# A spatial product in 2 x 3 by 3 x 3 blocks by 15 products instead of 2 x 2 by 7, with its sums of blocks of v accumulated in DRAM

## The chip, the core and the metric

The kernel runs on one core of a Trainium2 chip. The metric is the device time of one launch in microseconds (us), as the median of several runs. The profile is of one execution, and its times count from that execution's first instruction.

## The reference

There are three stages, of which the last holds the change. The first is the real part of a two-dimensional Fourier transform of `x` (4 batches, 3072 positions, 256 features). The second is a feed-forward layer with 2048 hidden features. The third is a gated layer in which positions are mixed:

```python
h = np.maximum(x @ w_in, 0.0)
u, v = (h[..., : d_ff // 2], h[..., d_ff // 2 :])          # 512 columns each
mu = np.mean(v, axis=-1, keepdims=True)
var = np.mean((v - mu) ** 2, axis=-1, keepdims=True)
v_n = (v - mu) / np.sqrt(var + 1e-06)
v_s = np.einsum('ts,bsd->btd', w_spatial, v_n) + b_spatial[None, :, None]
gated = u * v_s
return (gated @ w_out).astype(np.float32)
```

`w_spatial` is 3072 x 3072 and `v_n` is 3072 x 512 per batch. This "spatial product" is the largest piece of work of the kernel.

## The kernel before

**Three matmuls for one.** TensorE multiplies float32 operands that are split in two parts, `hi` (12 significant bits) and `lo` (the rest). `matmul3` (L160) issues three matmuls, hi by hi, hi by lo and lo by hi (L162 to L164). ScalarE makes `hi` by a copy (L829) and VectorE makes `lo` by a subtraction (L835).

**Fourier and feed-forward stages.** After the Fourier transform (L166 to L395) the loop at L721 walks over 16 blocks of 768 positions (4 batches of 4 blocks) in 8 steps each. Beside the matmuls of a block, the pieces of the block before are run: a `v_piece` (L631) makes 128 rows of v_n, a `u_piece` (L680) makes u, and both go to DRAM. A block has six v pieces, run one per step in the first six steps. For a v piece ScalarE applies the rectifier and sums the row (L658), GpSimd takes the mean (L660), ScalarE sums the squared deviations (L665), six small GpSimd instructions make 1/sqrt(var) (L666 to L671), and VectorE normalizes in place (`norm`, L674). The normalized tile is stored a step later by `run_norms` (L708): one DMA of 256 KB, issued by ScalarE (L710). Within `run_norms` the stores of the step before stand ahead of the new norms. For the last block the mean and the variance come from VectorE (L654, L655); its pieces are run by `finish` (L766) after the loop, among the first operands of the spatial product. Four buffers hold the v tiles.

**The spatial product.** Two batches make a pair. The product of a pair is cut into 2 x 2 blocks and done by seven products of sums of blocks (`PRODUCTS`, L38). Each product is made of units (L786): one unit is two blocks of 128 rows of s, one chunk `c` of 512 columns of t and all four blocks `j` of 128 features, 24 matmuls of 128x512. There are 2 pairs x 7 products x 3 chunks x 6 steps `p` = 252 units. Each unit needs its operand w, and each head `(product, p)` needs an operand v that all its chunks use.

An operand is made in steps that are written into the units ahead of its use: `load` (L807, SyncE, 512 KB per term into one of 7 `raw` buffers), `add` (L820, VectorE, one instruction per further term), `high` (ScalarE) and `low` (VectorE). For w they stand three, two, two and one units ahead (`operands`, L931). All engines work their queues in order, and SyncE goes on to the next load as soon as a `raw` buffer is free.

After the last step of a chunk, `collect` (L867) adds or subtracts its four accumulators (`sacc`) into the sums that the product belongs to, one VectorE instruction per accumulator and sum. Complete sums are multiplied by u (`gate_high`), split, and multiplied by w_out (`project`, L894) one block of 128 features at a time, in two PSUM banks of their own.

Of the kernel before, what the change touches and what calls it, by code (L numbers as in the profile page):

```python
# [13 lines left out]
ALU = mybir.AluOpType  # L14
# [23 lines left out]
PRODUCTS = [  # L38
# [7 lines left out]
]  # L46

# [29 lines left out]
def tables():  # L77
    """Twiddles of the folded transforms, by the shapes alone."""
# [31 lines left out]
def fourier_ffn_gated_kernel(ctx: ExitStack, tc: tile.TileContext, t, out: bass.AP):  # L110
# [7 lines left out]
    v_d = [[dram.tile([P, 6, HV], F32, name=f"v{b}{c}") for c in range(4)] for b in range(B)]  # L118
# [41 lines left out]
    def matmul3(acc, w, x, start, stop):  # L160
        """acc += w.T @ x from the split operands w = (hi, lo), x = (hi, lo)."""
        nc.tensor.matmul(acc, lhsT=w[0], rhs=x[0], start=start, stop=False)  # L162
        nc.tensor.matmul(acc, lhsT=w[0], rhs=x[1], start=False, stop=False)  # L163
        nc.tensor.matmul(acc, lhsT=w[1], rhs=x[0], start=False, stop=stop)  # L164

# [1 line left out]
    with ExitStack() as ph:  # L167
        pool = lambda n, **k: ph.enter_context(tc.tile_pool(name=n, reuse_waits="tile", **k))  # noqa: E731
# [48 lines left out]
        def rows384(b):  # L217
            """ce, so, co and se of row 384, in that order."""
# [29 lines left out]
        def row0(b):  # L248
            """Row 384 takes the rows that a sine of zero leaves free."""
# [5 lines left out]
        def lhs(b, sl):  # L255
            """The operands of the products along the sequence."""
# [374 lines left out]
    def v_piece(i, k):  # L631
# [461 lines left out]
```

## Time and profile before

| | |
|---|---|
| time of three runs | 2812.86, 2813.70 and 2813.86 us, median 2813.7 |
| span of the profiled execution, first to last instruction | 2809.1 us |
| what the median of the runs has beyond that span | 4.6 us |
| busy: PE, VectorE, ScalarE, GpSimd | 97%, 73%, 46%, 16% of the span |
| DMA: moved, mean rate | 438.91 MB, 156 GB/s |

The profile gives the profiled execution's span; its own time on the device's clock stands nowhere beside it, so the sum below is made against the span, and the 4.6 us around it are taken as unchanged. Busy shares are means over stages that differ much: the Fourier stage fills the first 200 us or so, the feed-forward stage goes to about 1276 us, and the spatial product from 1295 us to the end. GpSimd is busy in the first two stages alone.

### The profile page before, as it was taken

Reading aid. Unit: us, or ns where it says so; the run is one execution under the profiler, and the core shown is the slowest. Engines: PE = TensorE matmul, PEld = TensorE weight load, DVE = VectorE, ACT = ScalarE, POOL = GpSimd, SP = SyncE. Lnnn points to the kernel's source line nnn. Section 1 sums busy time; section 2 is a strip of 40 time slices with the busy share of each in tenths; the row PEclk is TensorE's granted clock in tenths of the full one; section 3 lists DMA queues with packets and bytes.
Section 4 is the critical chain, followed back from the end, with each engine's and each line's share of the span. In section 5 each row is a group of like instructions: output and inputs, shape, how many; then the busy total and the mean of one; then the engine's idle time right before and its main releaser. Section 6 shows DMA issues by size and latency. Waiting matters only on the chain.

```text
span 2809.1 us, 34578 instructions
## 1 busy us (share of the span) xinstructions
PE 2728.8 (97%) x13142; PEld 2410.1 (86%) x13142; DVE 2052.4 (73%) x2509; ACT 1301.6 (46%) x1652; POOL 453.8 (16%) x791
## 2 busy tenths in 40 slices
PE   5867999999999999999999999999999999999999
PEld 5757999999999999998888888888888888888887
DVE  8878888888888888886677665577645777646764
ACT  3455777777777777774323222233222232223332
POOL 5367222232222222222000000000000000000000
PEclk8979999999999999999999999999999999999999
DMA  5521111111111111117577775577746777736773
GB/s 226 174 80 42 54 58 54 57 54 60 57 58 54 57 58 54 49 64 273 171 254 247 262 257 173 188 241 265 257 165 195 242 262 261 245 131 230 249 255 118
DMA packets 158744, 438.91 MB, mean 156 GB/s; under 512 B 17753, under 2 KB 50538, under 8 KB 156914
## 3 DMA queue, kind: packets, MB, share of 16 engines
q1 hardware_dynamic: 122440, 380.04, 39.9%
q10 hardware_dynamic: 36138, 56.68, 5.5%
q8 instruction: 102, 1.67, 0.2%
q14 instruction: 64, 0.52, 0.1%
HBM read 367.41 MB, written 69.25 MB: 155 GB/s over the span
## 4 chain that ended last, share of the span: by engine, by line
PE 91%; DVE 4%; POOL 2%; DMA 1%; ACT 1%; issue 1%; ACTq 0%; SPq 0%; POOLq 0%; DVEq 0%
PE sacc L164 16%; PE sacc L163 16%; PE sacc L162 16%; PE acc L163 6%; PE acc L164 6%; PE acc L162 6%; PE po L163 3%; PE po L164 3%; PE po L162 3%; PE pu L162 2%; PE pu L164 1%; PE pu L163 1%; PE pv L164 1%; PE pe L163 1%; PE pe L164 1%; PE pe L162 1%
## 5 line engine op out<-in xcount | busy, mean ns | idle before, releaser
L164 PE MATMUL sacc<-whi,vlo 128*128 128x512 f32 x2016 | 786.9, 390 | 0.0
L162 PE MATMUL sacc<-whi,vhi 128*128 128x512 f32 x2016 | 784.9, 389 | 1.1 <-ACT uu L695 1.1
L163 PE MATMUL sacc<-wlo,vhi 128*128 128x512 f32 x2016 | 785.9, 390 | 0.0
L835 DVE TENSOR_TENSOR wlo<-raw,whi 128x1024 fp32r<-128x1024 f32 x252 | 308.6, 1224 | 489.0 <-PE sacc L163 321.1
L829 ACT CAST whi<-raw 128x1024 fp32r<-128x1024 f32 x252 | 265.1, 1052 | 586.9 <-DVE raw L823 440.2
L162 PEld LDWEIGHTS sacc<-whi,vhi 128*128 128x128 f32 x2016 | 378.5, 188 | 82.0 <-ACT uu L695 1.5
L163 PEld LDWEIGHTS sacc<-wlo,vhi 128*128 128x128 f32 x2016 | 378.3, 188 | 80.8
L164 PEld LDWEIGHTS sacc<-whi,vlo 128*128 128x128 f32 x2016 | 378.3, 188 | 79.3
L163 PE MATMUL acc<-glo,wo1h 128*128 128x384 f32 (+1 forms) x1024 | 350.4, 342 | 20.7 <-POOL glo L588 14.7
L162 PE MATMUL acc<-ghi,wo1h 128*128 128x384 f32 (+1 forms) x1024 | 348.5, 340 | 0.0
L164 PE MATMUL acc<-ghi,wo1l 128*128 128x384 f32 (+1 forms) x1024 | 348.4, 340 | 0.0
L588 DVE TENSOR_TENSOR glo<-h,ghi 128x1536 fp32r<-128x1536 f32 (+3 forms) x128 | 218.8, 1710 | 135.7 <-ACT ghi L581 135.7
L823 DVE TENSOR_TENSOR raw<-raw 128x1024 f32<-128x1024 f32 x240 | 288.3, 1218 | 0.0
L886 ACT CAST gh<-sum 128x512 fp32r<-128x512 f32 (+1 forms) x97 | 59.9, 618 | 380.0 <-DVE sum L884 380.0
L574 DVE SCALAR_TENSOR_TENSOR h<-e,h 128x1536 f32<-128x1536 f32 (+1 forms) x128 | 231.9, 1811 | 0.0
L563 ACT ACTIVATE e<-h 128x1536 f32<-128x1536 f32 (+1 forms) x128 | 190.0, 1485 | 87.7 <-DVE h L555 82.1
L163 PEld LDWEIGHTS acc<-glo,wo1h 128*128 128x128 f32 x1024 | 195.0, 190 | 25.5 <-POOL glo L588 17.1
L581 ACT CAST ghi<-h 128x1536 fp32r<-128x1536 f32 (+1 forms) x128 | 187.7, 1466 | 20.0 <-DVE h L574 20.0
L164 PEld LDWEIGHTS acc<-ghi,wo1l 128*128 128x128 f32 x1024 | 195.2, 191 | 0.0
L162 PEld LDWEIGHTS acc<-ghi,wo1h 128*128 128x128 f32 x1024 | 194.6, 190 | 0.1
L568 ACT ACTIVATE e<-e 128x1536 f32<-128x1536 f32 (+1 forms) x128 | 190.2, 1486 | 0.0
L554 DVE TENSOR_TENSOR h<-q,po 128x384 f32<-128x384 f32 (+1 forms) x256 | 142.1, 555 | 36.2 <-POOL glo L588 8.3
(196 smaller groups left out, 4141.7 us busy)
## 6 DMA issues: line engine op xcount, KB each, us to landing
raw<-in_wT SPq DMA_DIRECT2D x432, 512.0 KB, 4.6
raw<-v SPq DMA_DIRECT2D x144, 512.0 KB, 4.7
u<-uu ACTq DMA_DIRECT2D x128, 192.0 KB, 1.9
v<-v ACTq DMA_DIRECT2D x96, 256.0 KB, 2.9
u<-u SPq DMA_DIRECT2D x16, 1024.0 KB
q<-in_xq SPq DMA_DIRECT2D x12, 1032.0 KB
out<-sum SPq DMA_DIRECT2D x48, 256.0 KB, 2.1
u<-u SPq DMA_DIRECT2D x16, 512.0 KB, 4.4
```

The source lines that it names most:

```text
L162: nc.tensor.matmul(acc, lhsT=w[0], rhs=x[0], start=start, stop=False)
L163: nc.tensor.matmul(acc, lhsT=w[0], rhs=x[1], start=False, stop=False)
L164: nc.tensor.matmul(acc, lhsT=w[1], rhs=x[0], start=False, stop=stop)
L554: v.tensor_tensor(h[:, z, :n], q[:, :n], po[:, :n], op=ALU.add)
L563: nc.scalar.activation(e[:, :, :w], st[s]["h"][:, :, :w], AF.Relu, scale=-1.0)
L568: nc.scalar.activation(e[:, :, :w], e[:, :, :w], AF.Exp, scale=-1.0)
L574: nc.vector.scalar_tensor_tensor(out=h[:, :, :w], in0=e[:, :, :w], scalar=-1.0, in1=h[:, :, :w], op0=ALU.add, op1=ALU.max)
L581: nc.scalar.copy(st[s]["hi"][:, :, :w], st[s]["h"][:, :, :w])
L588: eng.tensor_tensor(st[s]["lo"][:, z, :w], st[s]["h"][:, z, :w], st[s]["hi"][:, z, :w].bitcast(F32), op=ALU.subtract)
L823: nc.vector.tensor_tensor(x, x, y, op=ALU.add if sg > 0 else ALU.subtract)
L829: nc.scalar.copy(hi, x)
L835: nc.vector.tensor_tensor(lo, x, hi.bitcast(F32), op=ALU.subtract)
```

## The change

The spatial product of a pair (2 batches by 3072 s by 3072 t) is cut into thirds of s and of t, not halves, and done by 15 products where 18 would be the plain number. A product now has 2 chunks of 512 columns and 4 steps, so a pair has 120 units, and both pairs 240.

- The table names for each product: a first and a second set of v blocks (blocks 0 to 2 are the thirds of the first batch, 3 to 5 of the second), the signed blocks of w, the sums that read the accumulator, and whether it continues on the accumulators that the product before left in PSUM ("running sums"). The products have 1, 3, 1, 2, 3, 1, 3, 1, 2, 3, 1, 3, 1, 2 and 2 terms of w.
- `V_SETS` are the 14 sets of v blocks that occur. Their sums are no longer made from loaded blocks: every normalized v tile is stored into each set that its block belongs to, five of them. The first block of a set is stored by SyncE, the others by GpSimd with an accumulating DMA. Of 480 stores of 256 KB, 224 are plain and 256 accumulate. Blocks 0 to 5 have 0, 3, 2, 3, 3 and 5 accumulating stores per tile.
- An operand v is then one load (two in the 14th product).
- The eight PSUM banks are the accumulators of the two chunks. `project` takes two banks of the chunk that is not being worked on, does all four blocks of features at once, and is put only where those banks hold no running sum (`idle`).
- There are 8 `raw` buffers in place of 7, loads stand one unit earlier (`LEAD`), the v operands have 5 buffers of each part and not 8, 11 buffers hold sums and u, and u is loaded by GpSimd. The bias is loaded in 24 pieces of 256 KB.

```diff
-VB = 8
+VB = 5
+KP = NT // 6
+MC = NCH // 3
...
 PRODUCTS = [
-    ([(1, 1, 0), (1, 1, 1)], [(1, 0, 0)], [(1, 1, 0), (-1, 1, 1)]),
...
+    ((1, 2, 4, 5), (), [(1, 1, 0)], [(1, 0, 0)], False),
+    ((1,), (), [(1, 1, 1), (-1, 0, 1), (-1, 1, 0)], [(1, 0, 1)], True),
+    ((4, 5), (), [(1, 2, 1)], [(1, 1, 1)], False),
+    ((2, 4, 5), (), [(1, 1, 0), (-1, 2, 1)], [(-1, 0, 1)], True),
+    ((2,), (), [(1, 0, 0), (1, 2, 1), (-1, 2, 0)], [(-1, 0, 0), (1, 1, 0)], True),
...
 ]
+NR = len(PRODUCTS)
+V_SETS = sorted({x for q in PRODUCTS for x in q[:2] if x})
...
         def norm():
             nc.vector.tensor_scalar(v, v, mean, y, op0=ALU.subtract, op1=ALU.mult)
-            stores.append((v_d[b][c][:, k], v))
+            third, at = divmod(6 * c + k, 2 * KP)
+            e = 3 * (b % 2) + third
+            for x in V_SETS:
+                if e in x:
+                    stores.append((v_d[b - b % 2, x, at // 2][:, at % 2], v, e != x[0]))
...
     def run_norms(n=None):
-        for x in stores:
-            nc.scalar.dma_start(*x)
+        for dst, v, more in stores:
+            if more:
+                nc.gpsimd.dma_start(dst, v, accum_op=ALU.add)
+            else:
+                nc.sync.dma_start(dst, v)
         stores.clear()
...
-    RAWS = 7
+    RAWS = 8
     WO2 = 6
-    NR = len(PRODUCTS)
-    KP = NT // 4
-    MC = NCH // 2
+    LEAD = 2
...
     def v_terms(i):
         b, r, p = heads[i]
...
+        return [(sg, v_d[b, x, p]) for sg, x in zip((1, -1), PRODUCTS[r][:2]) if x]
...
-        return p - 2 if r == 0 else MC * KP * r + (-14, -10, -5, -3, -1, 1)[p]
+        return p - 2 if r == 0 else MC * KP * r + (-6, -2, -1, 1)[p]
...
-                nc.sync.dma_start(
-                    u[:, :, t0 - first_t : t0 - first_t + w], u_d[b + n][blk][:, :, off : off + w]
-                )
+                src = u_d[b + n][blk][:, :, off : off + w]
+                nc.gpsimd.dma_start(u[:, :, t0 - first_t : t0 - first_t + w], src)
...
-        for key in steps.get(k + 1, []):
+        for key in steps.get(k + LEAD, []):
             load(key)
...
+    def bank(c, j):
+        return ps.tile([P, TC], F32, tag=f"a{c}{j}", name=f"a{c}{j}")
...
     for k, (b, r, c, p) in enumerate(units):
-        if projecting:
-            project(*projecting.pop())
+        if cutting:
+            key = cutting.pop()
+            pos = [bank(1 - c, 2 * turn + o) for o in range(2)]
+            turn = 1 - turn
+            for j in range(NJ):
+                project(key, pos, j)
+            put(key, pos)
         operands(k)
```

Two places show how instructions move. The first is GpSimd's queue at the end of the feed-forward stage, where the last block's v pieces are normalized. Before, the six instructions of one tile (`ve` to `y`) are followed by those of the next, and after the last tile by the conversion of w_out (`wo2r`):

```order
L666 TENSOR_SCALAR ve<-sums 128x1
L667 TENSOR_TENSOR y<-ve,nh 128x1
L668 TENSOR_TENSOR w<-y 128x1
L669 TENSOR_TENSOR w<-w,ve 128x1
L670 TENSOR_SCALAR w<-w 128x1
L671 TENSOR_TENSOR y<-y,w 128x1
L148 TENSOR_TENSOR wo2r<-wo2r,wo2b_13199 128x256
```

In the change, one tile's six instructions there are followed by five accumulating stores of an earlier tile, and only then by the next tile's:

```order
L684 TENSOR_SCALAR ve<-sums 128x1
L685 TENSOR_TENSOR y<-ve,nh 128x1
L686 TENSOR_TENSOR w<-y 128x1
L687 TENSOR_TENSOR w<-w,ve 128x1
L688 TENSOR_SCALAR w<-w 128x1
L689 TENSOR_TENSOR y<-y,w 128x1
L733 DMA v_1245_2_165<-v 128x512
L733 DMA v_245_2_173<-v 128x512
L733 DMA v_25_2_177<-v 128x512
L733 DMA v_35_2_185<-v 128x512
L733 DMA v_45_2_193<-v 128x512
```

What moved is the stores of v, from ScalarE's queue to GpSimd's, between the instructions that the next norms wait for. From the last two tiles of the block before on, the order on GpSimd is ten such stores, three tiles, five stores, one tile, five stores, one tile, five stores, the last tile.

The second place is VectorE's queue in the spatial product. Before, around a unit in which a chunk of a two-term product is collected (`sacc` is an accumulator):

```order
L876 TENSOR_TENSOR sum<-sum,sacc 128x512
L876 TENSOR_TENSOR sum<-bias,sacc 128x512
L835 TENSOR_TENSOR wlo<-raw,whi 128x1024
L884 TENSOR_TENSOR sum<-sum,u 128x512
L823 TENSOR_TENSOR raw<-raw 128x1024
L835 TENSOR_TENSOR wlo<-raw,whi 128x1024
L891 TENSOR_TENSOR gl<-sum,gh 128x512
```

In the change, around the end of the first chunk of the fifth product, which has three terms and is read by two sums (`a_` with a number is an accumulator):

```order
L843 TENSOR_TENSOR raw<-raw 128x1024 x2
L855 TENSOR_TENSOR wlo<-raw,whi 128x1024
L855 TENSOR_TENSOR vlo<-raw,vhi 128x1024
L843 TENSOR_TENSOR raw<-raw 128x1024 x2
L905 TENSOR_TENSOR sum<-sum,a_14104 128x512
L905 TENSOR_TENSOR sum<-bias,a_14104 128x512
```

What changed there is two additions per unit in place of one (`x2`), and v operands without any.

## Rows read from the trace of the kernel before

**Rows 1.** The page: busy us, share of the span and instructions of each engine.
```profile
PE 2728.8 (97%) x13142; PEld 2410.1 (86%) x13142; DVE 2052.4 (73%) x2509; ACT 1301.6 (46%) x1652; POOL 453.8 (16%) x791
```

**Rows 2.** Stretches: length, busy us (count) of PE, PEld, DVE, ACT, POOL, clock, DMA, GB/s.
```profile
1276.00:1297.30 21.30, 19.32 (x97) 16.80 (x95) 13.10 (x22) 11.51 (x19) 12.05 (x32) 1.00 0.90 288
1297.30:2809.00 1511.70, 1507.90 (x6624) 1242.33 (x6624) 970.02 (x1079) 436.62 (x490) 3.78 (x9) 1.00 0.66 224
```

**Rows 3.** Stretches of 200 us within the spatial product.
```profile
1400.00:1600.00 200.00, 200.00 (x880) 164.80 (x879) 142.32 (x153) 57.62 (x64) 0.00 (x0) 1.00 0.76 256
2400.00:2600.00 200.00, 200.00 (x880) 164.89 (x879) 112.77 (x123) 56.66 (x62) 0.00 (x0) 1.00 0.59 196
```

**Rows 4.** The page's groups: one of three rows of spatial matmuls.
```profile
L164 PE MATMUL sacc<-whi,vlo 128*128 128x512 f32 x2016 | 786.9, 390 | 0.0
```

**Rows 5.** Groups by line, 1400 to 2700 us: busy us, mean ns, idle before.
```profile
L835 DVE TENSOR_TENSOR wlo<-raw,whi 128x1024 fp32r<-128x1024 f32 x218 | 266.8, 1224 | 422.1 <-PE sacc L163 271.6 <-issue 98.8 <-ACT whi L829 36.7
L823 DVE TENSOR_TENSOR raw<-raw 128x1024 f32<-128x1024 f32 x218 | 261.5, 1218 | 0.0
...
L876 DVE TENSOR_TENSOR sum<-sum,sacc 128x512 f32<-128x512 f32 x180 | 115.8, 680 | 20.3 <-PE sacc L164 19.8
...
L884 DVE TENSOR_TENSOR sum<-sum,u 128x512 f32<-128x512 f32 x83 | 56.7, 684 | 0.0
```

**Rows 6.** The page's DMA issues: count, KB each, median us to landing.
```profile
raw<-in_wT SPq DMA_DIRECT2D x432, 512.0 KB, 4.6
raw<-v SPq DMA_DIRECT2D x144, 512.0 KB, 4.7
```

**Rows 7.** Stretches of 11, 22 and 44 us with the highest DMA rates.
```profile
1305.00:1316.00 11.00, 11.00 (x50) 9.10 (x49) 8.32 (x8) 4.17 (x5) 0.00 (x0) 1.00 1.03 408
1300.00:1322.00 22.00, 22.00 (x99) 18.22 (x98) 14.16 (x13) 10.43 (x11) 0.00 (x0) 1.00 0.96 360
2224.00:2268.00 44.00, 44.00 (x195) 36.15 (x194) 34.14 (x39) 14.82 (x18) 0.00 (x0) 1.00 0.84 295
```

**Rows 8.** Timeline of GpSimd, one feed-forward block: start us, us, what, idle before.
```profile
611.80 0.27 POOL L660 TENSOR_SCALAR mean<-sums 128x1 f32<-128x1 f32 x1 [14.60 <-ACT v L658]
...
615.22 1.67 POOL L670 TENSOR_SCALAR w<-w 128x1 f32<-128x1 f32 x1
...
643.23 1.64 POOL L660 TENSOR_SCALAR mean<-sums 128x1 f32<-128x1 f32 x1 [4.01 <-ACT v L658]
...
647.55 0.19 POOL L671 TENSOR_TENSOR y<-y,w 128x1 f32<-128x1 f32 x1
...
679.13 0.27 POOL L660 TENSOR_SCALAR mean<-sums 128x1 f32<-128x1 f32 x1 [14.60 <-ACT v L658]
```

**Rows 9.** Timeline of VectorE in the same block.
```profile
615.09 1.76 DVE L588 TENSOR_TENSOR glo<-h,ghi 128x1536 fp32r<-128x1536 f32 x1 [1.45 <-ACT ghi L581]
...
651.83 0.54 DVE L674 TENSOR_SCALAR v<-v,mean,y 128x512 f32<-128x512 f32 x1
```

**Rows 10.** Groups of GpSimd by line, 0 to 1300 us.
```profile
L588 POOL TENSOR_TENSOR glo<-h,ghi 128x770 fp32r<-128x770 f32 (+1 forms) x11 | 33.8, 3074 | 3.6 <-ACT ghi L581 3.6
...
L149 POOL TENSOR_TENSOR cv<-cv,cv 128x512 f32<-128x512 f32 x12 | 15.5, 1291 | 0.9
```

**Rows 11.** Timeline at the end of the feed-forward stage: a DMA issue, GpSimd.
```profile
1253.62 0.35 ACTq L710 DMA_DIRECT2D v<-v  x1
...
1270.64 0.19 POOL L671 TENSOR_TENSOR y<-y,w 128x1 f32<-128x1 f32 x1
1279.99 0.19 POOL L666 TENSOR_SCALAR ve<-sums 128x1 f32<-128x1 f32 x1 [9.16 <-DVE sums L655]
...
1281.71 0.19 POOL L671 TENSOR_TENSOR y<-y,w 128x1 f32<-128x1 f32 x1
```

**Rows 12.** Timeline there: the last norm on VectorE, the third unit on PE.
```profile
1298.49 0.55 DVE L674 TENSOR_SCALAR v<-v,sums,y 128x512 f32<-128x512 f32 x1 [1.53 <-POOL y L671]
...
1306.93 0.39 PE L162 MATMUL sacc<-whi,vhi 128*128 128x512 f32 x1
```

More of the change, by code (lines that the diff above doesn't have):

```diff
@@ L799, in w_terms @@
         return [
-            (sg, t["wT"][MC * m + c, :, 2 * (KP * half + p) : 2 * (KP * half + p) + 2])
-            for sg, half, m in PRODUCTS[r][1]
+            (sg, t["wT"][MC * m + c, :, 2 * (KP * third + p) : 2 * (KP * third + p) + 2])
+            for sg, third, m in PRODUCTS[r][2]
         ]
@@ L847, in fourier_ffn_gated_kernel, with reads, begun, load_bias @@
         steps.setdefault(v_step(i), []).append(("v", i))
-    us, sums, gates, projected = {}, {}, [], {}
-    def completed(r):
-        later = {x[1:] for q in PRODUCTS[r + 1 :] for x in q[2]}
-        return [x[1:] for x in PRODUCTS[r][2] if x[1:] not in later]
+    us, biases, sums, parts, gates, gated, cutting = {}, {}, {}, {}, [], [], []
+    def reads(r):
+        return [x[1:] for x in PRODUCTS[r][3]]
+    def begun(r):
+        return [x for x in reads(r) if all(x not in reads(q) for q in range(r))]
+    def completed(r):
+        return [x for x in reads(r) if all(x not in reads(q) for q in range(r + 1, NR))]
+    def load_bias(b, r, c):
+        for n, m in begun(r):
+            t0 = (MC * m + c) * TC
+            x = biases[b + n, MC * m + c] = gp.tile([P, TC], F32, tag="bias", bufs=1, name="bias")
+            nc.sync.dma_start(x, t["moe2_b_spatial"][t0 : t0 + TC].partition_broadcast(P))
     def load_u(b, r, c):
         for n, m in completed(r):
-            u = us[b + n, MC * m + c] = up.tile([P, NJ, TC], F32, tag="u", name="u")
+            u = us[b + n, MC * m + c] = cs.tile([P, NJ, TC], F32, tag="sum", name="u")
             first_t = t0 = (MC * m + c) * TC
@@ L907, in fourier_ffn_gated_kernel, with cut_high, cut_low, project @@
-    wo2_steps, wo2_raw = {}, []
+    def cut_high(key, j, cols=slice(0, TC)):
+        if cols.start == 0:
+            parts[key, j] = [gp.tile([P, TC], F32R, tag=f"g{x}", bufs=4, name=f"g{x}") for x in "hl"]
+        nc.scalar.copy(parts[key, j][0][:, cols], sums[key][:, j, cols])
+    def cut_low(key, j, cols=slice(0, TC)):
+        hi, lo = (x[:, cols] for x in parts[key, j])
+        nc.vector.tensor_tensor(lo, sums[key][:, j, cols], hi.bitcast(F32), op=ALU.subtract)
+    def project(key, pos, j, cols=slice(0, TC)):
+        for o, po in enumerate(pos):
+            matmul3(
+                po[:, cols],
+                [x[:, j, o * P : (o + 1) * P] for x in wo2],
+                [x[:, cols] for x in parts[key, j]],
+                j == 0,
+                j == NJ - 1 and cols.stop == TC,
+            )
@@ L909, in load_wo2, with put @@
+    def put(key, pos):
+        for o, po in enumerate(pos):
+            res = sums[key][:, o]
+            nc.scalar.copy(res, po)
+            nc.sync.dma_start(out[key][:, o], res)
+        del sums[key]
+    wo2_steps = {}
     def load_wo2(j):
-        if j == 0:
-            wo2_raw.append(up.tile([P, NJ, TC], F32, tag="u", name="wo2r"))
         raw = rp.tile([P, 4 * D], U32, tag="raw", bufs=RAWS, name=f"wo2b{j}")
@@ L924, in end, with continued, idle, gate @@
             split(wo2[0][:, j], wo2[1][:, j], rest)
-            if j == NJ - 1:
-                wo2_raw.clear()
         wo2_steps.setdefault(WO2 + j + 1, []).append(begin)
         wo2_steps.setdefault(WO2 + j + 2, []).append(end)
+    def continued(r):
+        return PRODUCTS[r % NR][4]
+    def idle(k):
+        _, r, c, p = units[k]
+        return p > 0 and not continued(r + (c == 1))
+    def gate(k):
+        for _ in range(2 if gates and gates[0][0][1] % MC == 1 or len(gates) > NJ or k >= NU - KP else 1):
+            if gates:
+                key, j = gates.pop(0)
+                multiply(key, j)
+                if j == NJ - 1:
+                    gated.append((key, k))
+                    del us[key]
+        if cutting:
+            for j in range(NJ):
+                cut_low(cutting[0], j)
     def operands(k):
@@ L934, in operands @@
             low(*key)
-        gate()
+        if gated and gated[0][1] < k and k + 1 < NU and idle(k + 1):
+            key, _ = gated.pop(0)
+            for j in range(NJ):
+                cut_high(key, j)
+            cutting.append(key)
+        gate(k)
         for key in steps.get(k, []):
@@ L998, in fourier_ffn_gated_kernel @@
             x()
-        if p == 4:
+        if p == 0 and not continued(r):
+            accs[c] = [bank(c, j) for j in range(NJ)]
+        if p == 2:
             load_u(b, r, c)
-        if p == 0:
-            accs = [ps.tile([P, TC], F32, tag="acc", name="sacc") for _ in range(NJ)]
+            load_bias(b, r, c)
         wh, wl = ready.pop(("w", k))
```

142 lines of the change are left out of this document (56 added, 86 removed), and 16 rows, old and new, of the table PRODUCTS.

## The prediction

> **What bounds the kernel now.** I read the page's busy shares first, then the stretches, then the groups by line, and last the timelines at the two places that the change loads. TensorE (PE) is busy for 97% of the span [rows 1], but that mean says little; the stretches say more. From 1297.3 us to the end PE is busy for 1507.9 of 1511.7 us [rows 2], so the spatial product is bound by PE and by nothing else. In a stretch of 200 us it starts 880 matmuls, early and late alike [rows 3]: one per 227.3 ns. The 390 ns in the groups is the length of one matmul, pipelined over the next, and is not its price [rows 4]. A unit of 24 matmuls is therefore 5.45 us. Next to that, VectorE is busy for 56 to 71% of these stretches and DMA for 59 to 76% [rows 3]: both have room, but not without end. In the feed-forward stage GpSimd is not a bound, but its short chain per v tile lies between ScalarE and VectorE, and the change puts its stores there.
>
> **What it saves.** The three rows of spatial matmuls hold 3 x 2016 = 6048 [rows 4]. After it there are 240 units of 24, or 5760; the order of PE's instructions shows the same 288 fewer, and `project` keeps its 576. 288 x 227.3 ns = **65.5 us**. That is the whole gain. The sum is made against the profiled execution's span of 2809.1 us, and the 4.6 us between that and the median stay.
>
> **What it adds in the spatial product.** The five products with three terms of w, in both pairs ten times eight units, are the tight ones. For each chunk of four units (21.8 us of PE) VectorE has 4 x (2 x 1.218 + 1.224) = 14.6 us for w, two v operands at 1.22, and four or eight collections at 0.68 [rows 5]: 19.8 or 22.5 us, and 2.7 us more where a finished sum is multiplied (four at 0.684, [rows 5]). That is 91 to 103% of PE's time; a chunk before or after, of one or two terms, has room to give back. DMA has 24 loads of w and 4 of v at 0.524 MB [rows 6] and a bias, 15.2 MB in 43.6 us, or 349 GB/s. The trace reached 408 GB/s over 11 us and 360 over 22 us; over 44 us the highest is 295, at 0.84 of DMA's time and with PE never idle [rows 7], so there it was the demand that set it. If 408 can be held the cost is 0; if 295 were the limit, a product would take 15.2 / 0.295 = 51.5 us, 7.9 us too long, or 79 us in ten. The need lies nearer to the rates of the full stretches, and eight buffers smooth it, so I take 1 us per such product: **10 us** (0 to 79). The conversion of w_out, which now lies beside the first of these products, is in that figure.
>
> **What it adds on GpSimd.** The trace has no DMA issued by GpSimd, so the price p of an accumulating store on that engine must be bounded. From below: a DMA issue on ScalarE's queue takes 0.35 us [rows 11]. From above: GpSimd's longest instruction on a tile takes 3.07 us [rows 10]. I take **p = 1.3 us**, the time of its pass over a tile of the same 128x512 [rows 10], because issuing also has to go through 128 rows, and that row too was measured beside a busy VectorE.
>
> *In the feed-forward loop.* A block takes 67.3 us on GpSimd's timeline (611.80 to 679.13), and the chain of one v tile 4.5 us (643.23 to 647.74), six tiles 27 us [rows 8]. So n stores per tile fit into a block while 6 n p is at most 40.3 us. For n = 3 that holds up to p = 2.2, for n = 5 up to 1.34. At 1.3 nothing is lost on the mean of a block. Step by step, five stores (6.5 us) stand in a gap of 4.0 us [rows 8], and the norm comes 4.1 us after its `y` (647.74 to 651.83, [rows 8, 9]). Six steps that are each 2.5 us late, less 4.1, could hold VectorE up by 11 us in the one full block with n = 5. Two steps without v tiles give that back, and PE has other matmuls queued: **3 us** (0 to 11).
>
> *At the end of the stage.* GpSimd is free at 1270.8 us and then has, by the order in the change, 25 stores and six tiles of 1.9 us (1279.99 to 1281.90) before the last `y` [rows 11]: 1282.3 + 25 p. Behind that on VectorE's queue stand the last norm (0.55 us) and the two lower parts of the third unit (2 x 1.22): 1285.3 + 25 p. PE started that unit at 1306.9 us [rows 12]. It comes late by 25 p - 21.6, at p = 1.3 by **11 us** (0 at 0.35; 55 at 3.07). Before, the last norm ran at 1298.5 us [rows 12], so there were 5.4 us to spare.
>
> **What costs nothing.** The 224 plain stores stand on SyncE's queue behind norms and ahead of the next block's loads, which stand there three steps before they are split. Loads of v fall from 144 to 128 and those of w rise from 432 to 480; this is in the rate above. VectorE loses its additions for v (nearly all of 60) and gains 60 for w. `project` waits for its split one unit after ScalarE, and its outgoing stores hold SyncE's queue until PE is done with it, ahead of loads that are needed two units later. u is loaded by GpSimd, which has 3.8 us of work in the whole stage [rows 2]. If these covers fail it shows as PE idle before `a` matmuls.
>
> **Sum.** 2813.7 - 65.5 + 10 + 3 + 11 = **2772 us**.
>
> **The rivals.** *Nothing is given back* (12%). GpSimd issues in under 0.87 us and DMA holds 400 GB/s: 2748 us. For it: PE never waited in the stretches of rows 7.
>
> *GpSimd becomes the bound of the feed-forward stage* (16%, slower). An instruction of 0.19 us takes 1.67 us when a two-operand instruction of VectorE began just before it (615.22 against 615.09 plus 1.76, [rows 8, 9]); GpSimd waits until that one is done. VectorE has two such instructions in every step. If a store is cut up by these waits, p grows. With p = 2.5: three stores per tile make a block 6 x 7.5 + 27 = 72 us, 4.7 too long in 8 blocks' worth of tiles (48 tiles), five make it 34.7 too long in 1.33 blocks (the other half of those tiles is the end), and the end costs 41: 38 + 46 + 41 + 10 - 65.5 = 69 us slower, 2883 us. It decides at p = 2.0, where end (28) and five-store tiles (26) and the 10 eat the gain; at 3.07 it is 244 us + 10 against 65.5. Against it: the same row of 1.3 us had VectorE beside it.
>
> The Trainium skill (SBUF — State Buffer, SBUF: two separate sides) has this as a rule: a DMA issued by GpSimd cannot write its descriptors while VectorE holds the shared port, and 620 ns alone become about 3100 ns beside it. The trace shows the wait, on a small instruction, but no such DMA; by the page's upper figure, as an estimate, the time would be near the far end above.
>
> *DMA is the bound in the products with three terms* (7%, slower). At 295 GB/s these give back 79 us: 2813.7 - 65.5 + 79 + 14 = 2841 us. For it: 44 us of higher demand are nowhere in the trace. Against it: 408.
>
> *The losses just cancel the gain* (5%): p near 2, or VectorE short by some 5 us in each product with three terms; 2814 us.
>
> That the change does not do what it says is ruled out by the order, which has the fewer matmuls.
>
> **How the numbers follow.** My forecast has 60%. It reaches from 2749 to about 2800, for p from 0.9 to 1.8 (at 1.8 the end costs 23 and the five-store tiles 18, with the 10 in the spatial product 51 us given back). Faster by over 0.2% (5.6 us, about what a measurement of this kernel can tell from no change): 60 + 12 = 72%. Same: 5%. Slower: 16 + 7 = 23%. The range goes from 2749, all of the gain, to 2836, which is p = 2.2 (end 33, five stores 35, three stores 0, and the 10) and a little more from DMA, so that it leaves out most of the third and about half of the fourth rival, some 18%. The forecast's own range is 2749 to 2800.
>
> **What would show it.** Right: in the spatial stage one matmul per 227 ns still and idle of PE before it of 10 us or less; DMA issues on GpSimd's queue near 1.3 us each; one gap of PE of about 10 us after the last pieces, ended by VectorE behind GpSimd. Wrong: PE idle in each feed-forward block, ended by VectorE's `glo`, with VectorE waiting for `y` (then p is above 2); or `raw` loads that take over 10 us to land and PE idle in the second, fifth, seventh, tenth and twelfth products (then DMA).

## The result and the profile after

The changed kernel takes 2839.3 us (median, 2835.7 to 2842.6) against 2813.3 for the kernel before beside it (2809.5 to 2813.9): a ratio of 1.0094, 95% interval 1.0080 to 1.0109, 26 us slower. The forecast was 2772.

From the page of the changed kernel's profile: PE's busy row, which answers to [rows 1], the queue of GpSimd's DMAs, which is new (packets, MB, share of the time of all 16 DMA engines), and the group of GpSimd's 256 accumulating stores (busy us, mean ns of one):

```profile
PE 2696.8 (95%) x12854; PEld 2373.8 (84%) x12854; DVE 2098.6 (74%) x2541; ACT 1308.7 (46%) x1676; POOL 703.8 (25%) x1079
...
q0 software_dynamic: 43520, 92.29, 18.0%
...
L733 POOL DMA_DIRECT2D v<-v x256 | 230.5, 1270 | 75.2 <-DVE v L692 46.4
```

The 288 matmuls are gone (13142 to 12854). With them PE's busy time should have fallen from 2728.8 [rows 1] by 65.5 to 2663.3 us; it is 2696.8. And PE's idle time, the span less the busy time, went from 80.3 to 2837.3 - 2696.8 = 140.5 us. So the ledger of the span is -65.5 + 60.2 idle + 33.5 longer matmuls = +28.2 us, and 2809.1 became 2837.3. Nearly all of the 33.5 is the clock. The view of the cores, of the changed kernel and of the kernel before (span, mean granted clock of TensorE):

```profile
core 0: 2837.3 us, clock 0.977
```
```profile
core 0: 2809.1 us, clock 0.988
```

What the clock lacks of 1 is 0.023 x 2837.3 = 65.3 us and 0.012 x 2809.1 = 33.7 us, 31.6 more (the sum takes PE as busy wherever the clock is low). The stretches, columns as in [rows 2, 3]:

```profile
1276.00:1340.00 64.00, 48.66 (x195) 40.91 (x196) 21.58 (x33) 20.51 (x32) 44.79 (x74) 0.84 1.09 256
...
1400.00:1600.00 200.00, 194.10 (x840) 159.17 (x839) 130.07 (x138) 52.88 (x54) 3.88 (x4) 0.98 0.71 241
...
2400.00:2600.00 200.00, 197.91 (x865) 163.14 (x864) 123.48 (x132) 58.87 (x65) 2.99 (x4) 0.99 0.69 236
```

Where 880 matmuls started in 200 us, there are now 840 and 865; and at the end of the feed-forward stage PE is idle for 15 of 64 us, at 0.84 of its clock. The groups of PE by line say who ended its idle time (the last column):

```profile
L181 PE MATMUL a<-wlo,vhi 128*128 128x512 f32 x1920 | 753.3, 392 | 18.0 <-DVE wlo L855 17.9
...
L180 PE MATMUL pu<-x2hi,wi2h 128*128 128x384 f32 x256 | 87.9, 343 | 10.4 <-ACT v L670 8.1 <-ACT uu L717 2.2
...
L181 PE MATMUL a<-gl,wo2h 128*128 128x512 f32 (+1 forms) x194 | 81.4, 419 | 19.6 <-DVE gl L921 19.6
```

Four places came out, by the start of each gap: the feed-forward loop (some 5 us: its last wait for `glo` is at 1276.5 us, and at 1271.7 in e1 below, a run without accumulating stores; nearly all of it is lost beside the one full block with five such stores per tile and the block after it, 140.3 us from 746.8 us on, 135.0 in e1), its end (15 us of idle, 1276 to 1333), the second product, beside which w_out is converted (13 us, 1373 to 1417), and from 1500 us on the projection's wait for `gl` (19.6) and waits for `wlo` (6). In or behind 12 of the 14 gaps of 2 us and more from 1276 us on the clock stands at its lower level, half the full one, for 3 to 10 us. One of them on PE's timeline (start, length, idle before):

```profile
1636.41 0.39 PE L182 MATMUL a<-whi,vlo 128*128 128x512 f32 x1
1637.13 0.47 PE L180 MATMUL a<-gh,wo2h 128*128 128x512 f32 x1 [0.34 <-ACT gh L917]
1640.57 0.80 PE L181 MATMUL a<-gl,wo2h 128*128 128x512 f32 x1 [2.96 <-DVE gl L921]
1641.17 0.63 PE L182 MATMUL a<-gh,wo2l 128*128 128x512 f32 x1
1641.59 0.63 PE L180 MATMUL a<-gh,wo2h 128*128 128x512 f32 x1
```

After 2.96 us without work matmuls start 0.42 us apart, not 0.227.

VectorE's timeline shows the ways in which it is late. In a product with three terms each unit has a wait for ScalarE between the additions and the lower part:

```profile
1623.66 1.23 DVE L855 TENSOR_TENSOR wlo<-raw,whi 128x1024 fp32r<-128x1024 f32 x1 [1.20 <-ACT whi L849]
1624.81 1.22 DVE L855 TENSOR_TENSOR vlo<-raw,vhi 128x1024 fp32r<-128x1024 f32 x1
1625.94 2.48 DVE L843 TENSOR_TENSOR raw<-raw 128x1024 f32<-128x1024 f32 x2
1629.61 1.23 DVE L855 TENSOR_TENSOR wlo<-raw,whi 128x1024 fp32r<-128x1024 f32 x1 [1.19 <-ACT whi L849]
...
1636.30 2.48 DVE L905 TENSOR_TENSOR sum<-bias,a 128x512 f32<-128x512 f32 x4 [1.94 <-DMA bias<-in_moe_b_spatial]
...
1956.22 4.86 DVE L905 TENSOR_TENSOR sum<-sum,a 128x512 f32<-128x512 f32 x8
1961.01 1.22 DVE L855 TENSOR_TENSOR wlo<-raw,whi 128x1024 fp32r<-128x1024 f32 x1
1962.14 1.22 DVE L855 TENSOR_TENSOR vlo<-raw,vhi 128x1024 fp32r<-128x1024 f32 x1
1963.28 1.28 DVE L912 TENSOR_TENSOR sum<-sum,u 128x512 f32<-128x512 f32 x2
1964.48 2.49 DVE L921 TENSOR_TENSOR gl<-sum,gh 128x512 fp32r<-128x512 f32 x4
```

The unit there is 1629.61 - 1623.66 = 5.95 us, against 5.45 of PE, and the bias is late on top. At 1956 it hasn't waited for anything: eight collections, two lower parts and two products stand ahead of the first `gl`, with it 8.9 us of work in a unit of 5.45, so the projection waits 2.9 us. Of the eight waits for `gl` four have eight collections ahead of them (10.0 us), two a late bias (5.9), and two lie in the fifteenth product, which has three terms (3.7).

### The profile page after: what moved, and what is told of

Read it like the earlier page. It is cut to its first block, busy times and chain, and to the rows that moved or that the text cites. A ratio compares the mean times of both kernels' runs of the same rounds, so it can differ in the third digit from the quotient of the medians.

```text
span 2837.3 us, 35269 instructions
## 1 busy us (share of the span) xinstructions
PE 2696.8 (95%) x12854; PEld 2373.8 (84%) x12854; DVE 2098.6 (74%) x2541; ACT 1308.7 (46%) x1676; POOL 703.8 (25%) x1079
## 4 chain that ended last, share of the span: by engine, by line
PE 72%; DVE 14%; DMA 4%; POOL 3%; issue 3%; ACT 3%; SPq 0%; ACTq 0%; DVEq 0%; POOLq 0%
PE a L181 13%; PE a L182 13%; PE a L180 13%; PE acc L181 5%; PE acc L182 5%; PE acc L180 5%; DVE raw L843 4%; DVE sum L905 2%; DVE vlo L855 2%; PE pv L181 1%; PE pv L180 1%; PE pv L182 1%; PE po L180 1%; PE pu L180 1%; PE po L181 1%
## 5 line engine op out<-in xcount | busy, mean ns | idle before, releaser
L181 PE MATMUL a<-wlo,vhi 128*128 128x512 f32 x1920 | 753.3, 392 | 18.0 <-DVE wlo L855 17.9
L182 PE MATMUL a<-whi,vlo 128*128 128x512 f32 x1920 | 752.8, 392 | 4.3 <-DVE vlo L855 4.3
L180 PE MATMUL a<-whi,vhi 128*128 128x512 f32 x1920 | 751.9, 392 | 1.6 <-ACT vhi L849 1.6
L855 DVE TENSOR_TENSOR wlo<-raw,whi 128x1024 fp32r<-128x1024 f32 x240 | 293.6, 1223 | 401.7 <-PE a L181 177.8
L181 PEld LDWEIGHTS a<-wlo,vhi 128*128 128x128 f32 x1920 | 362.8, 189 | 98.3 <-DVE wlo L855 22.1
L182 PEld LDWEIGHTS a<-whi,vlo 128*128 128x128 f32 x1920 | 363.1, 189 | 82.5 <-DVE vlo L855 6.6
L180 PEld LDWEIGHTS a<-whi,vhi 128*128 128x128 f32 x1920 | 363.2, 189 | 79.8 <-ACT vhi L849 3.4
L894 POOL DMA_DIRECT2D u<-u x32 | 24.0, 752 | 1275.2 <-DVE sum L912 1000.5
L843 DVE TENSOR_TENSOR raw<-raw 128x1024 f32<-128x1024 f32 x248 | 302.8, 1223 | 3.3
L733 POOL DMA_DIRECT2D v<-v x256 | 230.5, 1270 | 75.2 <-DVE v L692 46.4
L181 PEld LDWEIGHTS acc<-glo,wo1h 128*128 128x128 f32 x1024 | 195.1, 191 | 28.8 <-POOL glo L606 18.8
```

What stands on the lines that cost most here:

```text
L733: nc.gpsimd.dma_start(dst, v, accum_op=ALU.add)
L843: nc.vector.tensor_tensor(x, x, y, op=ALU.add if sg > 0 else ALU.subtract)
L855: nc.vector.tensor_tensor(lo, x, hi.bitcast(F32), op=ALU.subtract)
```

## The experiments

All start from the changed kernel. "Idle" is the profiled span less PE's busy time (140.5), "longer" is busy time over 2663.3 us (33.5); both are of one profiled execution, which can lie some 5 us from the median. The kernel before ran beside each group, at medians from 2811.3 to 2812.9 (2813.3 beside the changed kernel), so a difference of 2 us between groups says nothing.

| run | us, median | against 2839.3 | idle | longer |
|---|---|---|---|---|
| e1 no accumulating stores | 2807.6 | -31.7 | 124.8 | 22.3 |
| e2 w_out converted later | 2820.3 | -19.0 | 134.2 | 19.0 |
| e3 additions first | 2838.9 | -0.4 | 144.4 | 28.8 |
| e4 projection in mid-unit | 2824.0 | -15.3 | 128.2 | 30.4 |
| e5 bias earlier | 2826.7 | -12.6 | 134.2 | 27.2 |
| e6 halves | 2840.2 | +0.9 | 142.8 | 28.0 |
| e7 six v buffers at the end | 2837.1 | -2.2 | 144.0 | 30.3 |
| e8 and stores behind all else | 2832.7 | -6.6 | 144.5 | 22.7 |
| e9 = e2 + e4 + e5 | 2787.1 | -52.2 | 109.9 | 12.2 |
| e10 = e9 + e8 | 2786.1 | -53.2 | 109.6 | 12.1 |
| e11 = e10 + e6 | 2779.1 | -60.2 | 102.4 | 11.9 |
| e12 seven raw buffers | 2878.1 | +38.8 | 171.1 | 40.2 |
| e13 = e11 less 30 stores | 2759.2 | -80.1 | 89.8 | 3.9 |
| e14 last block apart | 2760.1 | -79.2 | 91.7 | 2.3 |
| e15 plain stores by GpSimd | 2820.9 | -18.4 | 135.6 | 24.5 |

**e1, no accumulating stores.**

```diff
-            if more:
-                nc.gpsimd.dma_start(dst, v, accum_op=ALU.add)
-            else:
+            if not more:
```

> The changed kernel without its 256 accumulating stores on GpSimd; the sums of blocks of v in DRAM then hold only their first block, so this part of the computation is left out, while every load, matmul and plain store stays. Theory (four losses of about 4 us in the feed-forward loop, 25 us at its end, 21 us beside the conversion of w_out and 39 us later, each made of idle time of TensorE and of the lower clock behind it): the first two vanish, 2839 - 29 = 2810 us, with 2800 to 2820. Rival, the end of the stage is late for its u tiles and its VectorE work and not for the stores: 2832 to 2839. Rival, the spatial product is short of DMA because stores of the stage are still draining: below 2795, since waits after 1400 us would go too.

2807.6 us, as the theory had it. The loop ends as early as before but for 1 us. All gaps between 1276 and 1340 us are gone, those after remain, so the spatial product isn't short because of stores.

**e2, w_out converted later.**

```diff
-    WO2 = 6
+    WO2 = 16
```

> The changed kernel with the loads and the conversion of w_out ten units later, beside the third product, which has one term of w, and no longer beside the second, which has three. Theory (VectorE and SyncE's queue can't take the conversion beside three terms; idle of 13 us and some 8 us of the lower clock behind it): 2839 - 21 = 2818 us. Rival, the clock does not matter: 2839 - 13 = 2826. Rival, loads for three terms are bound by DMA's rate: idle stays in the second product and the time stays within 2834 to 2842.

2820.3 us, near the theory. Of the 13 us of idle in the second product 3.4 remain. But of the 20.8 us between the profiled executions only 6.3 are idle; 14.5 are clock, and part of that is at places that the edit doesn't touch: it comes and goes with the same gap. Stretches of e2 and of the changed kernel, each with a gap of 2.9 us ended by `gl`:

```profile
1950.00:1960.00 10.00, 9.80 (x43) 8.07 (x44) 7.79 (x10) 4.26 (x6) 0.00 (x0) 1.00 0.66 204
```
```profile
1965.00:1975.00 10.00, 9.78 (x31) 7.82 (x32) 7.80 (x10) 3.04 (x4) 0.00 (x0) 0.69 0.39 141
```

43 matmuls at the full clock, 31 at 0.69. In e2 only 5 of its 13 gaps of 2 us and more from 1276 us on have the lower clock in or behind them. So a single gap can't be priced exactly.

**e3, additions first.**

```diff
+        for key in steps.get(k, []):
+            add(*key)
+            high(*key)
         for key in steps.get(k - 1, []) if k else []:
             low(*key)
...
         gate(k)
-        for key in steps.get(k, []):
-            add(*key)
-            high(*key)
```

> The changed kernel with the additions and upper parts of a unit's operands put ahead of the lower parts of the unit before, so that VectorE no longer waits 1.19 us per unit for ScalarE between them in products with three terms. Theory (that wait makes VectorE's unit 5.95 us against 5.45 of TensorE, so that the split of finished sums comes late for the projection): a good part of the 39 us after 1500 us comes back, 2810 to 2825. Rival (DMA's rate bounds those products, VectorE waits for loads as well): 2834 to 2842. Rival (the lower parts now come later and are what TensorE waits for): slower, 2845 to 2860.

No change. The wait for ScalarE is gone, but VectorE then waits up to 2.8 us for raw loads and 3.1 for the bias, and the projection waits 15.6 us for the upper part `gh`, whose sums come behind the additions. The theory fell; the time is that of the first rival, but the longest of the new waits, for `gh`, is of the edit's own making and is not in it. So the next runs took the parts singly.

**e4, projection in mid-unit.** `project` and `put` move behind the fourth of the eight `matmul3` of their unit:

```diff
+        for n, (z, j) in enumerate(order):
+            if n == NJ and due:
...
+                for x in range(NJ):
+                    project(due, pos, x)
+                put(due, pos)
```

> The changed kernel with each projection in the middle of its unit on TensorE, behind twelve matmuls of the unit (2.7 us), instead of ahead of them; VectorE's, ScalarE's and the DMAs' orders are the same. Theory (TensorE idles 2 to 3 us eight times because the split of the sum comes late by that much, and each such idle is followed by 3.4 to 6.8 us at the lower clock): the 19.6 us of idle go, and about 10 us of clock behind them, 2839 - 29 = 2810. Rival, the clock gives nothing back: 2839 - 19 = 2820. Rival, VectorE is short of time as a whole and the wait only moves to the next lower part of w: 2834 to 2842.

2824.0 us, nearest to the rival in which the clock gives nothing back: between the profiled executions 12.3 us are idle and 3.1 clock. All waits for `gl` are gone (19.6 us); 11 us come back as waits for `wlo`, the largest (3.6 and 3.9 us) just behind a late bias. Places like 1956, where no bias is late, are free. The edit does more than was expected of it: `put` now also stands behind the unit's `operands`, so that on ScalarE the outgoing copies come behind the upper parts, and on SyncE the outgoing stores behind the next loads. At the projection of 1965 the next load of w left at 1974.63 us behind the stores, and in e4 at 1970.58 ahead of them. No run parts the two, so the 15.3 us belong to both.

**e5, bias earlier.**

```diff
+        if p == 1:
+            load_bias(b, r, c)
         operands(k)
...
-            load_bias(b, r, c)
```

> The changed kernel with the bias tile loaded at the second of a chunk's four units, ahead of that unit's operand loads on SyncE's queue, and not at the third behind them. In the changed kernel's profile VectorE waits 9.3 us for it in five places, two of them ahead of a late split for the projection. Theory: at those places 3 us of idle of TensorE and some 3 of clock each go, and a little in the second product, 2839 - 8 = 2831 us, 2826 to 2834. Rival, VectorE is late there in any case by its own work: 2836 to 2842.

2826.7 us: more than the 8 us forecast, and within its range. VectorE no longer waits for the bias anywhere in the spatial product; half of the 12.6 us is idle (6.3) and half clock (6.3).

**e6, halves.** Additions, upper and lower part of three-term w in two halves:

```diff
+        for z in range(2) if len(more) == 2 else [slice(0, 2)]:
+            for sg, y in more:
+                nc.vector.tensor_tensor(x[:, z], x[:, z], y[:, z], op=ALU.add if sg > 0 else ALU.subtract)
```

> The changed kernel with the additions, the upper and the lower part of each w operand of three terms done in two halves of 128x512, so that ScalarE works on one half while VectorE adds the other. VectorE gets one more pass overhead per instruction (estimate 0.35 us a unit) and loses the wait of 1.19 us for ScalarE, 5.95 us per unit to some 5.1, below TensorE's 5.45. It leaves the order, the loads and the buffers as they are, unlike the run that put the additions first, in which w loads came later. Theory (VectorE with its wait is what TensorE is late by): most of the idle before projections (19.6 us) and lower parts of w after 1500 us goes, with clock behind it, 2839 - 30 = 2809, 2800 to 2818. Rival, loads from DRAM bound these products: 2834 to 2842, with VectorE's idle then before the additions, ended by DMA.

No change: this theory fell. VectorE's timeline in e6:

```profile
1632.43 1.46 DVE L859 TENSOR_TENSOR wlo<-raw,whi 128x512 fp32r<-128x512 f32 x2
...
1635.67 0.69 DVE L844 TENSOR_TENSOR raw<-raw 128x512 f32<-128x512 f32 x1 [0.29 <-DMA raw<-in_wT]
1637.19 2.02 DVE L844 TENSOR_TENSOR raw<-raw 128x512 f32<-128x512 f32 x3 [0.83 <-DMA raw<-in_wT]
1641.93 2.48 DVE L909 TENSOR_TENSOR sum<-bias,a 128x512 f32<-128x512 f32 x4 [2.72 <-DMA bias<-in_moe_b_spatial]
```

The wait for ScalarE is gone, and waits for the loads and the bias take its place.

**e12, seven raw buffers.**

```diff
-    RAWS = 8
+    RAWS = 7
```

> The changed kernel with seven buffers for raw operand tiles and not eight; more than eight don't fit into SBUF. Theory (a load of w starts when a buffer comes free, so the ring of buffers and the time to land set how early operands are there): more idle of TensorE in the products with three terms, 15 to 40 us slower, 2854 to 2879. Rival (DMA's rate sets it, or loads are early enough): within 4 us of 2839.

2878.1 us, at the upper end of the theory. The loads are no slower (median landing of w 5.0 us, 5.2 with eight, from the 68 loads in each trace that have one), and DMA moves a little less (239 GB/s from 1400 to 2700 us, 246 with eight). The groups of PE in e12 from 1340 us on:

```profile
L181 PE MATMUL a<-wlo,vhi 128*128 128x512 f32 x1897 | 746.6, 394 | 41.2 <-DVE wlo L855 41.2
...
L181 PE MATMUL a<-gl,wo2h 128*128 128x512 f32 (+1 forms) x194 | 81.4, 420 | 24.0 <-DVE gl L921 24.0
```

A buffer fewer costs 39 us: with seven the ring of buffers, not the rate, sets when operands are there. With eight SyncE too waits for a buffer ahead of most loads (706.8 us in 207 waits for `wlo` from 1340 us on, 763.8 in 211 with seven), but whether a ninth would give anything back no run shows.

**e7 and e8, the end of the stage.** Six buffers of their own for the last block's v tiles; in e8 also the last block's stores behind all of GpSimd's other work:

```diff
+        if i == len(blocks) - 1 and k >= 0:
+            v = vend[0].tile([P, HV], F32, tag="vend", bufs=6, name="v")
...
+            if more and vend:
+                after_all.append((dst, v))
```

> The changed kernel with six buffers of their own for the v tiles of the last block, and the same order on every queue. Theory (ScalarE waits for buffers that accumulating stores hold until they land): the 10.4 us of idle that end with ScalarE's v go, and some 4 us of clock, 2839 - 14 = 2825. Rival, the order on GpSimd (stores ahead of the chain for y) holds the last norms as late as before, and TensorE waits for the third unit instead: 2834 to 2842.

> The same six buffers, and the last block's 30 accumulating stores issued by GpSimd after all its other work of the stage. Theory: nothing of the stage's end waits for a store any more, 2839 - 25 = 2814, and no less than the 2808 of the run without accumulating stores. Rival, the load on DMA alone delays u tiles and the first operands, wherever the stores stand: 2825 to 2835.

In the changed kernel ScalarE waits for v buffers that stores hold until they land:

```profile
1312.92 0.60 ACT L670 ACTIVATE v<-pv 128x512 f32<-128x512 f32 x1 [7.49 <-DMA v<-v]
...
1320.21 0.60 ACT L670 ACTIVATE v<-pv 128x512 f32<-128x512 f32 x1 [6.32 <-DMA v<-v]
```

With six buffers (e7) that goes, and the last norm waits for GpSimd, as the prediction had it; VectorE in e7:

```profile
1323.86 0.55 DVE L696 TENSOR_SCALAR v<-v,sums,y 128x512 f32<-128x512 f32 x1 [7.67 <-POOL y L693]
1324.32 1.22 DVE L860 TENSOR_TENSOR wlo<-raw,whi 128x1024 fp32r<-128x1024 f32 x1
```

In e8 that goes too, but PE then waits 6.8 and 8.3 us for `wlo` at 1364 and 1379, with VectorE behind ScalarE and ScalarE behind the loads of w_out (12.0 us in two waits; 8.1 in e7, 2.1 in the changed kernel). PE's idle time from the end of the loop to the third unit falls from 14.2 us to 4.6 (e7) and 4.9 (e8), and from there to 1500 us it rises from 13.6 to 25.3 and 23.5. Both times came out as the rivals had them; e7 can't be told from no change.

**e15, plain stores by GpSimd.**

```diff
-                nc.gpsimd.dma_start(dst, v, accum_op=ALU.add)
+                nc.gpsimd.dma_start(dst, v)
```

> The changed kernel with GpSimd's 256 stores overwriting and not accumulating (so the sums of blocks of v are left out); the same number, size, engine and order. Theory (it is the accumulation in DMA that costs, not the issue): the stage's end loses most of its 16 us of idle and the clock behind it, 2839 - 22 = 2817, 2812 to 2824. Rival (the order on GpSimd, stores ahead of the chain for y, and their issue): 2834 to 2842. If it lies between, both count.

2820.9 us, within the theory: 18.4 of e1's 31.7 us are the accumulation, the other 13 the stores as such. Of the stage's end the theory said too much, since 9.2 of the 14.2 us of idle before the third unit remain; the loop's 5 us are gone. The stores by line in the changed kernel (issue, min, median and max in ns; who waited; landing), then in e15, and the queue in e15 and e1:

```profile
L733 POOL DMA_DIRECT2D v<-v x256: 856/1186/2616, 378.6 to 1348.2; - x128
...
  ACT v L670: 17.7, 4
...
DMA to landing us min/median/max: 3.9/6.5/19.3
```
```profile
L733 POOL DMA_DIRECT2D v<-v x256: 539/539/771, 379.5 to 1322.4; - x128
...
DMA to landing us min/median/max: 2.4/2.8/10.5
```
```profile
q0 software_dynamic: 27136, 92.29, 9.0%
```
```profile
q0 software_dynamic: 6656, 25.17, 2.6%
```

For the same bytes GpSimd's queue takes 18.0% of all 16 DMA engines' time when it accumulates and 9.0% when not; 2.6% are u. So an accumulating store of 256 KB takes 0.154 x 2837.3 / 256 = 1.71 us of all engines, a plain one 0.064 x 2823.4 / 256 = 0.71 us.

**e9, e10, e11, the edits together.**

> Three edits that alone gave 19, 15 and 13 us, together: w_out converted beside the third product, the projection in the middle of its unit, the bias tile one unit earlier. Theory (the losses stand in a row in one TensorE stream, so gains add, except at the two places where the bias and the projection share a wait): 2839 - 47, and up to 7 less, 2792 to 2799, faster than the kernel before by some 15 us. Rival (VectorE has too little time as a whole, and each wait that goes comes back at the next lower part of w): 2805 to 2820.

> The same three and the six buffers with the late accumulating stores at the end of the feed-forward stage. These alone gave 6.6 us, since TensorE then waited 6.8 and 8.3 us in the second product, where w_out was converted. Theory (that conversion took the gain back, and it has moved): 18 us less than with three edits, 2774 to 2784. Rival (stores that are still landing delay the first operand loads, wherever the conversion stands): within 8 us of the run with three.

> The same five and the operands of three terms in two halves. Alone the halves changed nothing: VectorE's wait for ScalarE went, and waits for the bias and for raw loads came in its place. Theory A (the bias was what took it back): 5 to 12 us less than with five edits. Theory B (loads of w take it back, since VectorE, now earlier, meets them before they have landed): within 4 us of the run with five, with VectorE's idle ahead of the additions, ended by DMA.

Three edits give 52 us, more than their sum of 47, and below the forecast range. The surplus is idle time and not clock: against the changed kernel e9 has 30.6 us less idle (e2, e4 and e5 together 24.9) and 21.3 less of longer matmuls (together 23.9). Of the waits for `wlo` after 1500 us, which e4 alone had raised to 17.2, 8.8 are left. The late stores add nothing: PE's idle time before the third unit falls from 15.7 to 4.8 us, and from there to 1500 us it rises from 0.6 to 10.8. VectorE in e10 waits for w, while GpSimd's stores follow one another at the pace at which earlier ones land:

```profile
1386.22 1.23 DVE L850 TENSOR_TENSOR raw<-raw 128x1024 f32<-128x1024 f32 x1 [4.89 <-DMA raw<-in_wT]
```
```profile
1324.32 0.86 POOL L1022 DMA_DIRECT2D v<-v  x1 [1.78 <-DMA v<-v]
...
1369.79 0.86 POOL L1022 DMA_DIRECT2D v<-v  x1 [1.70 <-DMA v<-v]
```

The halves, worth nothing alone, now give 7 us, as theory A had it. That it was the bias that had hidden them is argued from e6's timeline; no run has the halves and the bias alone.

**e13 and e14, without the late stores.** e13 is e11 with `pass` in place of `after_all.append((dst, v))`. In e14 the last block of v is stored once and loaded as a second term where a set has it:

```diff
+            if last:
+                stores.append((v5_d[at // 2][:, at % 2], v, False))
...
+        more = [(1, v5_d[p])] if b == B - 2 and p and 5 in PRODUCTS[r][0] else []
```

> The five edits and the halves, with the last block's 30 accumulating stores left out (the sums in DRAM then lack that block; this part of the computation is missing). Theory (accumulating stores keep all DMA engines busy: put late they followed one another every 2.6 us until 1371 us, and w loads took 12.5 us to land, so TensorE waited 10.3 us in the second product and ran 13.6 us at the lower clock): 2779 - 17 = 2762, 2757 to 2768. Rival (the second product's loads are late because three terms are more than DMA or the ring of buffers gives there): 2774 to 2782.

> The five edits and the halves, but the last block of v is stored once, plainly, and not accumulated; in the second pair, the five products whose sum has it load it as a second term for three of their four operands (15 more loads and 15 more additions on VectorE, in place of 30 accumulating stores). Theory: as without those stores, 2762, and up to 8 us for the loads and additions, 2762 to 2770. Rival (the ring of raw buffers has no room for the extra loads): idle before a<-whi or a<-wlo in the second pair, 2775 to 2790.

2759.2 us, within the theory, and 2760.1, 2 us below its range. So the late stores were what made the second product's loads late, and they can be avoided. The 12.5 us to land in e13's expectation is the middle of two loads only, 10.6 and 14.3 us. e14 leaves nothing out and is faster than both kernels: 0.9813 of the kernel before, interval 0.9798 to 0.9828. Its page, and its groups of PE from 1276 us on:

```profile
PE 2665.6 (97%) x12854; PEld 2352.7 (85%) x12854; DVE 2143.8 (78%) x2844; ACT 1329.5 (48%) x1772; POOL 671.5 (24%) x1049
```
```profile
L182 PE MATMUL a<-wlo,vhi 128*128 128x512 f32 x1920 | 749.2, 390 | 1.9 <-DVE wlo L868 1.9
...
L182 PE MATMUL a<-gl,wo2h 128*128 128x512 f32 (+1 forms) x194 | 75.6, 390 | 0.0
```

PE's busy time is within 2.3 us of the 2663.3 that the saved matmuls promise. A stretch of 44 us of e14 in the second product, columns as in [rows 7]:

```profile
1345.00:1389.00 44.00, 44.00 (x196) 36.44 (x195) 38.29 (x57) 15.46 (x21) 0.00 (x0) 1.00 0.91 328
```

DMA moves 328 GB/s there with PE never idle, so the 295 of [rows 7] was no limit.

## Why the prediction was wrong, point by point

- **What it saves: right.** 288 matmuls, 65.5 us; e14's busy time shows it.
- **The price of a store: the step "I take p = 1.3 us" failed, and its agreement with the page is luck.** 1270 ns is the mean length of an issue, but issues in a row overlap: each that began beside an earlier one ended 0.89 us after it (median), and GpSimd was busy with all 256 for 230.5 us, 0.90 us each. 1270 ns is what the prediction itself says of the 390 ns of a matmul: a length, not a price. With 0.90 its own formula makes the end of the stage 1 us late. So the rival in which GpSimd bounds the feed-forward stage (p of 2.0 and more) fell, and the loop lost some 5 us against 3, where the prediction looked for it. The Trainium skill (SBUF — State Buffer, SBUF: two separate sides) has its 620 ns and 3100 for a VectorE copy in a mode that takes both ports, and for a VectorE instruction with two inputs it has a block only against GpSimd work that reads SBUF. The stall of [rows 8, 9] fits the latter; a plain issue, 539 to 771 ns in the same place beside the same VectorE work, shows none, so the rival was no case of that rule.
- **The end of the stage: the step "it comes late by 25 p - 21.6" failed.** It gave a store a price on GpSimd's queue and none in DMA. By the measured p it comes to 1 us; lost were 15 us of idle and the clock behind it, and e1 puts loop and end together at 31.7, against the 14 of the sum. The wait named (norms behind stores) is real, as e7 shows, but a longer one stood ahead of it: v buffers held until stores of 6.5 us had landed. The sign named, a gap of PE ended by VectorE behind GpSimd, came as one of 8.1 us ended by ScalarE behind a v buffer. Thirty such stores are 30 x 1.71 = 51 us of all DMA engines, and wherever they were put something else then came late: the last norm and the loads of w_out (e7), the loads of w_out (e8), the loads of w (e10). The Trainium skill (Collectives: The Full Stack, The bandwidth ceiling: the fold count and why AG ≠ RS ≠ AR) says of a ring of cores that a reduction in DMA reads two sources and so runs at half a copy's rate; here 1.71 against 0.71 us is a factor of 2.4, and no run shows whether the cause is the same.
- **The products with three terms: the step "I take 1 us per such product" failed, in three places.** *"The conversion of w_out ... is in that figure"*: it alone cost 13 us of idle, of which e2 took 9.5. *"A bias"*, counted only in bytes: it came late on SyncE's queue, 12.6 us (e5). *"Eight buffers smooth it"*: with one fewer the kernel loses 39 us more (e12), so there was little to smooth with. There are also six such products and not five: the fifteenth, listed with two terms under the change, has three (the 480 loads of w need them), so the term would have been 12 us. VectorE's 91 to 103% left out the four `gl` (2.5 us) and the 1.19 us per unit that it waits for ScalarE; that wait was worth nothing by itself (e3, e6) and 7 us at the end (e11).
- **"What costs nothing": the step "`project` waits for its split one unit after ScalarE" failed.** It named no cover for the unit in which eight collections, or a late bias, stand ahead of the split. 19.6 us of idle; the wait is gone in e4. The plain stores on SyncE's queue did cost next to nothing: e1, which keeps them, ends the loop 1 us later than the kernel before.
- **A term that was not there: the clock.** Every matmul was priced at 227.3 ns, the price in a stream without gaps. The longer matmuls are 33.5 us in all, half as much again on the 60.2 of idle.
- **The rivals.** The bound by DMA's rate came nearest in time (2841), but for another reason: e14 moves more over 44 us than the rival allows, with PE never idle. Of the changed kernel's loads of w the trace has the landing of 68: 5.2 us at the median, against 4.6 [rows 6]. Three of those 68 took over 10 us, the sign that was named, and with the late stores of e10 both of the two that the trace has between 1340 and 1395 us.

So 65.5 us were gained and 60.2 + 33.5 given back. The place of each loss is shown by a run that takes it away, and e14 takes away nearly all of them; that eight raw buffers are too few, and which part of e4's gain is the projection's place, is argued. How the clock's part divides over the gaps stays open, since like gaps did and didn't lower it.

## What to carry to other kernels

When a stream that never waited is shortened, price the gaps that appear by what follows them as well: here 60 us of idle brought 33 us of slower matmuls. An accumulating DMA is to be charged three times, to the engine that issues it, to the buffer that it holds until it lands, and to all DMA engines; here the last couldn't be moved away, only avoided. The mean length of an instruction is its price only where one doesn't overlap the next; busy time by count is safer. A wait counted at nothing needs its own sum at the worst unit (what stands ahead on that engine's queue, against one unit's time), not the mean; and a fix that shows nothing alone should be tried again when the wait in front of it is gone.

## What the runs showed of the hardware

- Of the 14 gaps of PE of 2 us and more from 1276 us on in the changed kernel 12 came with stretches at 1.2 GHz, 0.42 us from one 128x512 matmul to the next and not 0.227; in e2 only 5 of 13 did, and a gap of the same length at the same place was not among them.
- An accumulating store of 256 KB from GpSimd took its queue 0.90 us (its length, 0.86 to 2.62 us, is more where issues overlap) and landed in 6.5 us (median), a plain one took 0.56 (143.0 us for 256) and landed in 2.8; in DMA time it is 1.71 against 0.71 us of all 16 engines.
- In e10 nine accumulating stores issued one behind the other ran free (8.0 us), and from then on each waited 0.4 to 2.2 us for an earlier one to land: one every 2.5 us from 1324 to 1370 us, with the w loads beside them. The wait is at a semaphore; whether the chip or the program sets this depth isn't shown.
- Over 44 us DMA moved 328 GB/s beside a PE that was never idle (e14).
